# Two tiles of w2 on 32 partitions, in loads of six rows: a change to the last feed-forward of a two-layer decode kernel

## The chip, the cores and the metric

The kernel runs on one core of a Trainium2 chip. The metric is the device time of one execution in microseconds; lower is better. The core has TensorE (PE in the profile, its weight loads PEld), VectorE (DVE), ScalarE (ACT), GpSimd (POOL) and SyncE (SP), which issues nearly all DMAs here, and 16 DMA engines that move the data.

## The reference

Two layers of the same weights, each an attention block and a gated feed-forward, for 4 batch rows of one token (B=4, D=512, 32 query heads over 8 key heads, 4096 cached positions of 128 values, F=1792), all in float32:

```python
x = x + attention(layernorm(x), k_cache, v_cache, wq, wo)
x = x + (silu(h @ w1) * (h @ w3)) @ w2        # h = layernorm(x)
# ... and both lines once more, with the same caches and weights
```

Both layers read the whole k and v caches, 67 MB each. Together with the weights the core reads 298.33 MB from HBM and does little arithmetic on each byte.

## The kernel before

**The plan of loads.** All big operands go through one SBUF buffer, `arena` (218 units of 1 KB on each of 128 partitions). Lines 86 to 159 write out a list, `plan`, of every load of the run in the order in which SP is to issue them: source, size, and the pieces that the consumers will ask for. `cache()` cuts one head's k or v (64 units) into parts, `weights()` cuts a weight matrix. `pump()` (L164) walks the list: it asks `take()` (L56) for a free stretch of the arena, issues the DMA from SP (L183), and stops when nothing fits. `done()` (L196) frees a load's stretch when all of its pieces have been used, and pumps again. So the order of all big transfers is the order of the plan, and what holds a load back is free space in the arena.

**The units.** One unit is 256 floats, 1 KB per partition. An ordinary load lies on 128 partitions. A tile of w2 is 128 rows of h times 512 columns, two units, 256 KB; w2 has 14 of them (`WT`).

**The loads of the last layer.** After the last heads come w1 and w3 in two parts each (16 units, 16, 12, 12) and then w2. The first tile of w2 does not come on 128 partitions. It comes as `w2s`: 16 rows (`FEW`) of 16 KB each. Row r of it holds rows r, 16+r, 32+r and so on of the tile, side by side, so that the 256 KB lie on 16 partitions in 16 units of arena. Lines 150 to 153 cut them into four loads of four rows each (rows i, i+4, i+8, i+12), and lines 155 to 158 put one of them ahead of each of the four parts of w1 and w3. `pump()` takes 16 units for all of them at the first and has GpSimd clear them on all 128 partitions (L175); the loads themselves are issued at L177. The other 13 tiles follow as one list of parts of 8, 8, 4, 4 and 2 units (L159), that is 4, 4, 2, 2 and 1 tiles.

**The last feed-forward on TensorE.** `product()` makes w1 and w3 times x in two column parts (L530). After the first part of the gated h is there, L583 transposes it, and L586 cuts the 128 rows that belong to tile 0 into eight groups of `FEW` values on `FEW` partitions. `few(0, 4)` and `few(4, 8)` multiply these with the eight blocks of `w2s`, ahead of the last part of w3 and behind it; `columns()` (L555) writes four matmuls for each block or tile, one for each 128 output columns (L557). Then the loop at L615 takes tiles 1 to 13 as their loads land, with two idle matmuls (`busy`) after tiles 4 and 8. L670 copies the sum out of PSUM and L671 stores it.

**Where the first layer's FF uses w2.** Layer 0 loads all 14 tiles of w2 on 128 partitions in pairs and multiplies them in `down()` (L548).

**The k loads at the change of layers.** For the second head of layer 1 line 144 cuts k into loads of 8, 8, 8, 8, 16 and 16 units, for the third head into two of 32, and it leaves the later ones whole.

Of the kernel before, what the change touches and what calls it, by code (L numbers as in the profile page):

```python
# [13 lines left out]
B, D, HQ, HKV, SK, DH, F = 4, 512, 32, 8, 4096, 128, 1792  # L14
LAYERS = 2
REP = HQ // HKV
P = 128
# [6 lines left out]
FA = 2 * P  # L24
FB = FJ - FA
WT = 14
FEW = 16
EPS = 1e-5
SCALE = DH ** -0.5

KB = 256
# [7 lines left out]
def tile_decode_layers(ctx: ExitStack, tc: tile.TileContext, x, kt, v, wq, wo, w1, w3, w2, w2s, out):  # L39
# [46 lines left out]
    plan = []  # L86

    def load(src, per, keys, at=None):
        plan.append((src, per, keys, at))

    def cache(which, layer, g, parts, skip=0):
        src = (kt if which == "k" else v)[g]
        r = 8 * skip
        for n in parts:
            at = KEPT + r if (which, layer, g) in (("v", 0, TURN), ("k", 1, TURN - 2)) else None
            load(src[:, r * KB:(r + n) * KB], 8, [(which, layer, g, r // 8 + j) for j in range(n // 8)], at)
            r += n

    def weights(name, src, layer, parts, per, at=None, first=0):
        r = 0  # L100
        for n in parts:
            load(src[:, r * KB:(r + n) * KB], per, [(name, layer, first + r // per + j) for j in range(n // per)],
                 None if at is None else at + r)
            r += n

    order = [list(range(HKV)), list(reversed(range(HKV)))]
# [34 lines left out]
    ring["to"] = len(plan) - 1  # L141
    cache("k", 1, TURN, (8, 8, 16), SPLIT)
    for n in range(1, HKV):
        cache("k", 1, order[1][n], {1: (8, 8, 8, 8, 16, 16), 2: (32, 32)}.get(n, (64,)))
        if n > 1:
            cache("v", 1, order[1][n - 1], (32, 32) if n == HKV - 1 else (64,))
    cache("v", 1, 0, (32, 16, 16))


    side = iter([(w2s[i::4], slice(i, FEW, 4)) for i in range(4)])  # L150

    def aside():
        plan.append((*next(side), "few", None))

    for part, per, at in (("a", 4, 0), ("b", 3, 16)):
        for name, w in (("w1", w1), ("w3", w3)):
            aside()
            weights(name + part, w[:, at * KB:(at + 4 * per) * KB], 1, (4 * per,), per)
    weights("w2", w2[:, 2 * KB:], 1, (8, 8, 4, 4, 2), 2, None, 1)  # L159

    state = {"next": 0}
    where, left = {}, {}
# [29 lines left out]
    def loaded(*key):  # L192
        a, n, _ = where[key]
        return arena[:, a * KB:(a + n) * KB]

    def done(*key):  # L196
        i = where[key][2]
        k, a, n = left[i]
        left[i] = (k - 1, a, n)
        if k == 1:  # L200
            give(a, n)
            pump()
# [12 lines left out]
    few = const.tile([P, 4], F32, name="few")  # L215
# [37 lines left out]
    a = scaled  # L253
# [6 lines left out]
    hT = qT.rearrange("p h c -> p (h c)")[:, 0:(WT + 8) * B].rearrange("p (m b) -> p m b", b=B)  # L260
# [28 lines left out]
    def busy(n=1):  # L289

        while n > 0:
            w = min(n, 2)
            nc.tensor.matmul(m_ps[0:32, (4 - w) * P:], rows, ident.unsqueeze(1).broadcast_to([P, w, P]),  # L293
                             start=True, stop=True)
            n -= w
# [13 lines left out]
    def squares():  # L309
        sq = work.tile([P, KC, B], F32, name="sq", bufs=1)  # L310
        nc.vector.tensor_tensor(sq, xc, xc, op=ALU.mult)
        return sq

    def deviation(sq, m):
        var = small("var")
        nc.vector.scalar_tensor_tensor(sq, m, 1.0, pick, op0=ALU.mult, op1=ALU.mult, accum_out=var)
        nc.vector.tensor_scalar(var, var, EPS, None, op0=ALU.add)
        rstd = small("rstd")
        nc.gpsimd.tensor_tensor(rstd, var, half, op=ALU.pow)
        return rstd  # L320
# [164 lines left out]
    def pair(i, left, w, first, last):  # L485

        for n in range(2):
            for e in range(2):
                r = 32 * (2 * n + (e ^ (i % 2)))
                nc.tensor.matmul(x_ps[r:r + B, e * 256:e * 256 + 256], left(2 * i + n), w(n)[:, e * 256:e * 256 + 256],  # L490
                                 start=first, stop=last)
# [30 lines left out]
    def feed_forward(layer, mean):  # L522
        keep = layer < LAYERS - 1
        h = p[:, 0:FJ]

        def product(name, ps, lo, n, fill=(0, 0, 0, 0), ks=range(KC)):
            for k in ks:
                w = loaded(name, layer, k)
                for j in range(4):
                    nc.tensor.matmul(ps[32 * j:32 * j + 32, lo:lo + n], x32[:, k, :], w[:, j * n:(j + 1) * n],  # L530
                                     start=(k == 0), stop=(k == KC - 1))
                done(name, layer, k)
                busy(fill[k] if keep else 0)

        def gate(lo, n):
            a = h[:, lo:lo + n]
            nc.scalar.activation(a, s_ps[:, lo:lo + n], AF.Sigmoid, scale=rstd)
            nc.vector.scalar_tensor_tensor(a, s_ps[:, lo:lo + n], rstd, a, op0=ALU.mult, op1=ALU.mult)

        def join(lo, n):  # L540
            a = h[:, lo:lo + n]
            nc.vector.scalar_tensor_tensor(a, o_ps[:, lo:lo + n], rstd, a, op0=ALU.mult, op1=ALU.mult)

        def tiles(lo, n):
            slots = t_ps.rearrange("p i (j b) -> p (i j) b", j=4)
            nc.vector.tensor_copy(hT[:, lo:lo + n, :], slots[:, lo:lo + n, 0:B])

        def down(i):  # L548
            ws = [loaded("w2", layer, 2 * i + n) for n in range(2)]
            pair(i, lambda m: hT[:, m, :], lambda n: ws[n], i == 0, i == WT // 2 - 1)  # L550
            for n in range(2):
                done("w2", layer, 2 * i + n)
            busy((1, 2, 2, 2, 1, 2, 0)[i])

        def columns(rows, m, w, last=False):  # L555
            for k in range(KC):
                nc.tensor.matmul(x_ps[32 * k:32 * k + B, 0:P], hT[rows, m, :], w[rows, k * P:(k + 1) * P],  # L557
                                 start=False, stop=last)

        def few(lo, hi):  # L560
            for u in range(lo, hi):
                at = (where["few"] + 2 * u) * KB
                columns(slice(0, P), WT + u, arena[:, at:at + 2 * KB])

        sq = squares()
        product("w1a", s_ps, 0, FA, (0, 0, 2, 0))
        rstd = deviation(sq, total(flat(sq)))
        mean()
        if not keep:
            nc.vector.tensor_tensor(xt, xc, mu.unsqueeze(1).broadcast_to([P, KC, B]), op=ALU.add)  # L570
        product("w3a", o_ps, 0, FA, (2, 2, 2, 2))
        if not keep:
            for k in range(KC):
                nc.tensor.matmul(x_ps[32 * k:32 * k + B, 0:P], xt[:, k, :], ident, start=True, stop=False)
            busy(4)
        gate(0, FA)
        join(0, FA)
        product("w1b", s_ps, FA, FB, (1, 1, 1, 1))
        if keep:
            gate(FA, FB)  # L580
            nc.scalar.activation(spare, half, AF.Exp)
        for i in range(2):
            nc.tensor.transpose(t_ps[:, i, :], h[:, i * P:(i + 1) * P], ident)  # L583
        if not keep:
            for u in range(8):
                nc.tensor.matmul(t_ps[0:FEW, 2, B * u:B * u + B], h[0:32, FEW * u:FEW * u + FEW], ident[0:32, 0:B],  # L586
                                 start=True, stop=True)
            busy()
        tiles(0, 8)
        if not keep:  # L590
            nc.vector.tensor_copy(hT[0:FEW, WT:WT + 8, :], t_ps[0:FEW, 2, 0:8 * B].rearrange("p (u b) -> p u b", b=B))
            gate(FA, FB)
            few(0, 4)
        product("w3b", o_ps, FA, FB, (1, 2, 1, 1), range(0, 2))
        if keep:
            down(0)
        product("w3b", o_ps, FA, FB, (1, 2, 1, 1), range(2, KC))
        join(FA, FB)

        def tail_tiles():  # L600
            nc.tensor.transpose(t_ps[:, 2, :], h[:, FA:FA + P], ident)
            for u in (0, 64):
                nc.tensor.matmul(t_ps[u:u + 64, 3, 0:64], h[u:u + 64, FA + P:FJ], ident[u:u + 64, u:u + 64],
                                 start=True, stop=True)
            tiles(8, 6)

        if keep:
            for i in range(1, WT // 2):
                if i == 4:
                    tail_tiles()  # L610
                down(i)
            return
        few(4, 8)
        tail_tiles()
        for m in range(1, WT):  # L615
            columns(slice(0, P), m, loaded("w2", layer, m), m == WT - 1)
            done("w2", layer, m)
            if m in (4, 8):
                busy(2)
# [92 lines left out]
```

## Time and profile before

| | |
|---|---|
| median of 3 runs | 704.82 us (704.65 to 704.92) |
| profiled execution | 704.5 us, of which its span is 702.7 us |
| read from HBM | 298.33 MB, 425 GB/s over the span |
| PE busy, PEld, DVE, ACT, POOL | 402.9, 135.5, 85.2, 38.0, 7.0 us |

The span is the time from the first to the last instruction of the profiled execution. Busy times of engines overlap. Lines such as L557 are lines of the kernel before.

### The profile page before, as it was taken

The numbers are of one execution on the slowest core, as the hardware profiler recorded it, in microseconds if no ns is written. First come the engines' busy times: TensorE is split into PE (matmuls) and PEld (weight loads), VectorE is DVE, ScalarE is ACT, GpSimd is POOL, SyncE is SP. The second block draws the span as 40 slices with busy tenths as digits, with TensorE's granted clock in tenths as the row PEclk, the third lists the DMA queues.
The fourth block names the chain that finished last, engine by engine and source line by source line (L and its number), as shares of the span: only waits on it lengthen the run. The fifth ranks groups of instructions, "written<-read, shape, count | busy, mean of one in ns | idle before, by whom it ended". The sixth has DMA issues, their size and how long they took to land. (4 is left out here: it accounts for less than half of the span.)

```text
span 702.7 us, 7079 instructions
## 1 busy us (share of the span) xinstructions
PE 402.9 (57%) x3172; PEld 135.5 (19%) x3172; DVE 85.2 (12%) x291; ACT 38.0 (5%) x87; POOL 7.0 (1%) x12
## 2 busy tenths in 40 slices
PE   2555453555555454447888884365564545467677
PEld 1112011111111111112233321011120111122234
DVE  2001010101001010101111111020010101010111
ACT  0000000000000000102001000000000000000100
POOL 0000000000000000000000000000000000001000
PEclk9986787767778777779999997588787878788899
DMA  9999999999999999999999999999999999999997
GB/s 418 429 407 466 422 422 422 451 426 425 430 451 422 429 430 444 425 421 427 415 405 408 416 437 441 448 425 419 452 433 425 422 451 426 433 419 432 420 426 287
DMA packets 13174, 298.85 MB, mean 425 GB/s; under 512 B 1608, under 2 KB 1736, under 8 KB 6216
## 3 DMA queue, kind: packets, MB, share of 16 engines
q1 hardware_dynamic: 13008, 298.39, 99.2%
q8 instruction: 25, 0.41, 0.2%
q14 instruction: 6, 0.04, 0.0%
q10 hardware_dynamic: 135, 0.01, 0.0%
HBM read 298.33 MB, written 0.07 MB: 425 GB/s over the span
## 5 line engine op out<-in xcount | busy, mean ns | idle before, releaser
L462 PE MATMUL o_ps<-arena 128*32 128x512 f32 x1024 | 143.1, 706 | 149.6 <-DMA arena<-in_v 137.7
L415 PE MATMUL s_ps<-arena,qpad 128*32 128x512 f32 x1020 | 147.5, 732 | 92.0 <-DMA arena<-in_kt 92.0
L462 PEld LDWEIGHTS o_ps<-arena 128*32 128x32 f32 x1024 | 37.0, 127 | 253.3 <-issue 224.3
L415 PEld LDWEIGHTS s_ps<-arena,qpad 128*32 128x32 f32 x1020 | 39.3, 131 | 183.9 <-issue 176.4
L471 DVE SCALAR_TENSOR_TENSOR p<-o_ps,parts,p 128x512 f32<-128x512 f32 x16 | 12.0, 751 | 267.4 <-PE o_ps L462 267.4
L425 DVE TENSOR_REDUCE top<-s_ps 128x1 f32<-128x512 f32 x16 | 11.1, 691 | 196.6 <-PE s_ps L415 196.6
L469 ACT ACTIVATE p<-o_ps,parts 128x512 f32<-128x512 f32 x16 | 11.0, 687 | 188.5 <-PE o_ps L462 182.3
L293 PE MATMUL m_ps<-ident,rows 128*32 128x256 f32 (+1 forms) x84 | 20.9, 352 | 0.0
L353 PE MATMUL o_ps<-arena,xpad 128*32 128x512 f32 x112 | 15.5, 676 | 7.8 <-DMA arena<-in_wq 7.8
L448 PE MATMUL t_ps<-ident,p 128*128 128x128 f32 x64 | 10.9, 295 | 13.5 <-ACT p L442 13.5
L475 PE MATMUL t_ps<-ident,p 128*128 128x128 f32 x64 | 10.5, 287 | 13.9 <-DVE p L471 13.8
L435 ACT ACTIVATE f<-d 128x1 f32<-128x1 f32 x16 | 3.2, 203 | 251.0 <-DVE d L433 251.0
L497 PE MATMUL x_ps<-arena,qT 128*4 128x512 f32 x112 | 13.8, 592 | 5.1 <-DVE qT L483 3.6
L442 ACT ACTIVATE p<-s_ps,top 128x512 f32<-128x512 f32 x16 | 10.9, 684 | 75.9 <-PE t_ps L475 75.9
L449 DVE COPY arena<-t_ps 128x512 f32<-128x512 f32 x16 | 11.1, 691 | 9.3 <-PE t_ps L448 9.3
L475 PEld LDWEIGHTS t_ps<-ident,p 128*128 128x128 f32 x64 | 6.7, 140 | 28.0 <-DVE p L471 28.0
L448 PEld LDWEIGHTS t_ps<-ident,p 128*128 128x128 f32 x64 | 7.0, 145 | 22.2 <-ACT p L442 19.2
L293 PEld LDWEIGHTS m_ps<-ident,rows 128*32 128x32 f32 x84 | 9.0, 110 | 9.0 <-issue 3.5
L530 PE MATMUL s_ps<-arena,xpad 128*32 128x192 f32 (+1 forms) x128 | 7.9, 359 | 1.5 <-DMA arena<-in_w 1.5
L530 PE MATMUL o_ps<-arena,xpad 128*32 128x192 f32 (+1 forms) x128 | 8.1, 359 | 1.0 <-DMA arena<-in_w 0.9
L490 PE MATMUL x_ps<-arena,qT 128*4 128x256 f32 x88 | 6.6, 379 | 2.4 <-DMA arena<-in_w 1.7
L353 PEld LDWEIGHTS o_ps<-arena,xpad 128*32 128x32 f32 x112 | 3.5, 121 | 17.2 <-DMA arena<-in_wq 8.7
(108 smaller groups left out, 147.6 us busy)
## 6 DMA issues: line engine op xcount, KB each, us to landing
arena<-in_v SPq DMA_DIRECT2D x5, 4096.0 KB, 38.4
arena<-in_w SPq DMA_DIRECT2D x17, 512.0 KB, 9.3
arena<-in_kt SPq DMA_DIRECT2D x2, 4096.0 KB, 18.7
arena<-in_wq SPq DMA_DIRECT2D x1, 7168.0 KB
arena<-in_kt SPq DMA_DIRECT2D x6, 1024.0 KB, 11.2
arena<-in_kt SPq DMA_DIRECT2D x3, 2048.0 KB, 16.7
arena<-in_wo SPq DMA_DIRECT2D x1, 4096.0 KB, 24.0
arena<-in_v SPq DMA_DIRECT2D x2, 2048.0 KB, 36.9
```

The costliest lines, as they stand in the source:

```text
L293: nc.tensor.matmul(m_ps[0:32, (4 - w) * P:], rows, ident.unsqueeze(1).broadcast_to([P, w, P]), start=True, stop=True)
L353: nc.tensor.matmul(ps[32 * k:32 * k + 32, :], xpad[:, 32 * k + lo:32 * k + lo + 32], w[:, k, :], start=first, stop=last)
L415: nc.tensor.matmul(s_ps[32 * b:32 * b + 32, :], qpad[:, 32 * b + lo:32 * b + lo + 32], k[:, j, :], start=(blk == 0), stop=(blk == NB - 1))
L425: nc.vector.tensor_reduce(top[:, 0:1], s_ps, axis=AX.X, op=ALU.max, negate=True)
L448: nc.tensor.transpose(t_ps[:, i, :], p[:, i * P:(i + 1) * P], ident)
L449: nc.vector.tensor_copy(pT.rearrange("p i r -> p (i r)"), t_ps.rearrange("p i r -> p (i r)"))
L462: nc.tensor.matmul(o_ps[32 * b:32 * b + 32, :], pT[:, i, 32 * b:32 * b + 32], w[:, b, :], start=(i == 0), stop=(i == NI - 1))
L469: nc.scalar.activation(p, o_ps, AF.Copy, scale=st["parts"][:, 0:1])
L471: nc.vector.scalar_tensor_tensor(p, o_ps, st["parts"][:, 1:2], p, op0=ALU.mult, op1=ALU.add)
L475: nc.tensor.transpose(t_ps[:, j, :], p[:, j * P:(j + 1) * P], ident)
L497: nc.tensor.matmul(x_ps[r:r + B, :], left(2 * i + n), w(n), start=first, stop=False)
L530: nc.tensor.matmul(ps[32 * j:32 * j + 32, lo:lo + n], x32[:, k, :], w[:, j * n:(j + 1) * n], start=(k == 0), stop=(k == KC - 1))
```

## The change

Two tiles of w2 instead of one are laid as rows of 16 KB: the first 256 rows of h's first quarter, tiles 0 and 4, on 32 partitions (`FEW` = 32). Each of the eight blocks that `few()` multiplies now holds 32 rows. The 32 rows come in six loads, five of six consecutive rows and one of two: two loads ahead of the first part of w1 and two ahead of the first part of w3, one ahead of each second part. `TILE` keeps the list of w2's tiles in the order 0, 4, 1, 2, 3, 5, ...; the array in HBM is laid in that order, `down()` and the last loop look up h through it. The last loop runs over 12 tiles, loaded in parts of 8, 8, 6 and 2 units: 4, 4, 3 and 1 tiles. The third and fourth load of k for the second head of layer 1 become one of 16 units. The number of DMAs of the program is the same: two more for `w2s`, one less for w2, one less for k.

```diff
-FEW = 16
+FEW = 32
+TILE = (0, 4, 1, 2, 3, *range(5, WT))
...
-        cache("k", 1, order[1][n], {1: (8, 8, 8, 8, 16, 16), 2: (32, 32)}.get(n, (64,)))
+        cache("k", 1, order[1][n], {1: (8, 8, 16, 16, 16), 2: (32, 32)}.get(n, (64,)))
...
-    side = iter([(w2s[i::4], slice(i, FEW, 4)) for i in range(4)])
-
-    def aside():
-        plan.append((*next(side), "few", None))
+    side = [slice(6 * i, min(6 * i + 6, FEW)) for i in range(6)]
+
+    def aside(n):
+        for _ in range(n):
+            part = side.pop(0)
+            plan.append((w2s[part], part, "few", None))
...
-            aside()
+            aside(2 if part == "a" else 1)
             weights(name + part, w[:, at * KB:(at + 4 * per) * KB], 1, (4 * per,), per)
-    weights("w2", w2[:, 2 * KB:], 1, (8, 8, 4, 4, 2), 2, None, 1)
+    weights("w2", w2[:, 4 * KB:], 1, (8, 8, 6, 2), 2, None, 2)
...
-            pair(i, lambda m: hT[:, m, :], lambda n: ws[n], i == 0, i == WT // 2 - 1)
+            pair(i, lambda m: hT[:, TILE[m], :], lambda n: ws[n], i == 0, i == WT // 2 - 1)
...
-        for m in range(1, WT):
-            columns(slice(0, P), m, loaded("w2", layer, m), m == WT - 1)
+        for m in range(2, WT):
+            columns(slice(0, P), TILE[m], loaded("w2", layer, m), m == WT - 1)
...
-        "w2": lay(np.concatenate([full, rest], axis=1)).reshape(P, WT * D),
-        "w2s": lay(w2j[0, :P].reshape(8, FEW, D).transpose(1, 0, 2)).reshape(FEW, 8 * D),
+        "w2": lay(np.concatenate([full, rest], axis=1)[:, list(TILE)]).reshape(P, WT * D),
+        "w2s": lay(w2j[0, :FEW * 8].reshape(8, FEW, D).transpose(1, 0, 2)).reshape(FEW, 8 * D),
```

## The prediction

> **What bounds the kernel now.** I read the page first: busy shares, the forty slices, the DMA queues.
>
> ```profile
> span 702.7 us, 7079 instructions
> ...
> PE 402.9 (57%) x3172; PEld 135.5 (19%) x3172; DVE 85.2 (12%) x291; ACT 38.0 (5%) x87; POOL 7.0 (1%) x12
> ...
> DMA  9999999999999999999999999999999999999997
> ...
> q1 hardware_dynamic: 13008, 298.39, 99.2%
> ...
> q10 hardware_dynamic: 135, 0.01, 0.0%
> ```
>
> The sixteen DMA engines are full in 39 of 40 slices, and SP's queue q1 alone fills 99.2% of their time; TensorE is busy 57%. The kernel lasts as long as the transfers last, plus what follows the last byte. An edit counts only if it changes the bytes (this one doesn't), starves the engines, moves work between them at the end, or lengthens what comes behind the last landing. So I went to the end: the chain of waits in order of time, then the share of busy DMA engines in short windows.
>
> ```profile
> 683.82 15.04 DMA arena<-in_w
> 698.86 0.04 issue
> 698.90 0.62 PE x_ps L557 x16
> 699.52 0.02 issue
> 699.55 0.45 PE x_ps L557 x8
> 699.99 0.02 issue
> 700.02 0.29 DVE p L670
> ```
>
> ```profile
> 660.00:680.00 20.00, 14.43 (x117) 5.51 (x117) 3.70 (x11) 3.24 (x7) 0.00 (x0) 1.00 0.99 420
> ...
> 694.00:695.00 1.00, 1.00 (x37) 0.96 (x34) 0.18 (x1) 0.00 (x0) 0.00 (x0) 1.00 0.98 373
> 695.00:696.00 1.00, 0.49 (x6) 0.01 (x1) 0.00 (x0) 0.00 (x0) 0.00 (x0) 1.00 0.75 299
> 696.00:697.00 1.00, 0.62 (x24) 0.61 (x28) 0.00 (x0) 0.00 (x0) 0.00 (x0) 1.00 0.75 293
> 697.00:698.00 1.00, 1.00 (x34) 0.71 (x26) 0.00 (x0) 0.00 (x0) 0.00 (x0) 1.00 0.57 229
> 698.00:699.00 1.00, 0.38 (x16) 0.10 (x8) 0.00 (x0) 0.00 (x0) 0.00 (x0) 1.00 0.42 145
> 699.00:700.00 1.00, 0.93 (x24) 0.34 (x19) 0.00 (x0) 0.00 (x0) 0.00 (x0) 1.00 0.00 0
> ```
>
> In a window row the last columns are granted clock, DMA share and GB/s. The chain says that the load ahead of the last one ends the last long wait: it lands at 698.86, sixteen matmul records (two tiles) take 0.62, the last tile 0.45 from 699.55, then copy and store. The windows show how the engines run out: 0.75 of 16 is 12 still busy from 695 to 697, 0.57 is nine until 698, and by 699 nothing moves. So four engines finish about 695, three more about 697, nine between 698.3 and 699.
>
> This gives a first bound. The idle shares from 694 to 699 add up to 0.02 + 0.25 + 0.25 + 0.43 + 0.58 = 1.53 us. Were all sixteen to finish together, the last byte would land 1.53 us earlier: 0.22% of 704.8. No rebalancing of the end can give more. About 0.2%, 1.4 us, is also what a measurement of this kernel can tell from no change.
>
> **Which engines carry the 16 KB rows.** A load of 120 rows (x, line 210, the only load of queue q10) left 135 packets: 120 rows and 15 closing ones, so it ran on 15 engines, one closing packet for each. With the same count q1's 13,008 are 90 transfers of 128 rows (128 + 16 each), x's first 8 rows (8 + 8), and 32 for the four w2s loads, which is four times 4 + 4. So a load of four rows ran on four engines, one row each; six rows should run on six engines and two on two, since a number of rows that is no power of two (120) was split by its largest divisor. [...]
>
> The trace also holds each packet's start and length. Chained end to start, an estimate of mine beside the windows, they give sixteen ends: four chains hold all sixteen 16 KB rows, so it was the same four engines each time, and they end near 696.9, 696.9, 697.1 and 699.05. Of the twelve others four end at 694.5 to 696.0, and eight at 698.3 to 698.8. That fits the windows.
>
> **The parts, priced.** A 16 KB row: 420 GB/s at a share of 0.99 is 26.5 GB/s for an engine, so 0.62 us. A w2 tile on 128 partitions is 8 rows of 2 KB, 16 KB, on every engine: from 695 to 696, 299 GB/s on 12 engines is 24.9 each, 0.66 us.
>
> *All sixteen engines* lose one tile: -0.66. *The four engines with rows now* carry 4 rows, 2.48 us. After it the first two of the six carry 5 + 1 rows and the next two 5: +1.24 - 0.66 = +0.58 for two and +0.62 - 0.66 = -0.04 for two. *Two engines more* take 5 rows: +3.10 - 0.66 = +2.44. If these two are among the early four, they end at 696.9 to 698.4; if among the late eight, at 701.2. *The ten others* gain 0.66; the late eight end at 697.6 to 698.2.
>
> So all hangs on two identities. That the two newcomers are early I take as likely: the early eight are the four row carriers (without rows they would end near 694.4 to 696.6) and four others, and engines side by side in the order of use are likelier to share the cause than to be split by it. Which of the carriers ends at 699.05 decides the last byte: third or fourth in the order 699.0, first or second 699.6. By count that is even. I take 699.0, because one of the four early chains without rows is late in its group too (696.0, the others 694.5 to 695.0): if lateness touches neighbours, the pair is the fourth carrier and the first newcomer.
>
> *Behind the last byte.* The last two loads are now three tiles and one, where they were two and one. A tile costs 0.31:
>
> ```profile
> 697.65 0.64 PE L557 MATMUL x_ps<-arena,qT 128*4 128x128 f32 x16
> 698.90 1.04 PE L557 MATMUL x_ps<-arena,qT 128*4 128x128 f32 x24 [0.62 <-DMA arena<-in_w]
> ```
>
> Two tiles in 0.64. The last tile still lands about 0.65 behind the load before it; two tiles just filled that gap (698.90 to 699.52), three need 0.94. So the last tile starts 0.3 later: +0.3. Twelve tiles instead of thirteen spare TensorE 0.31, but ahead of a wait, so nothing.
>
> *SP's queue.* The issues of the last loads:
>
> ```profile
> 644.01 0.70 SPq L177 DMA_DIRECT2D arena<-in_w2s  x1
> 644.76 0.43 SPq L183 DMA_DIRECT2D arena<-in_w  x1
> 645.24 0.61 SPq L177 DMA_DIRECT2D arena<-in_w2s  x1
> 645.96 0.38 SPq L183 DMA_DIRECT2D arena<-in_w  x1
> 654.47 0.60 SPq L177 DMA_DIRECT2D arena<-in_w2s  x1
> 664.20 0.33 SPq L183 DMA_DIRECT2D arena<-in_w  x1
> 669.09 0.60 SPq L177 DMA_DIRECT2D arena<-in_w2s  x1
> 674.03 10.60 SPq L183 DMA_DIRECT2D arena<-in_w  x6
> ```
>
> The steps 9.73, 4.89 and 4.94 are the times of a load of 4 MB and two of 2 MB: v's last three parts, which land one after the other. Counted along the plan, each issue waits until the load eight places ahead has landed. With two more w2s loads in front, w3's first part moves from 645.96 to 664.2 and w1's second part from 664.20 to 674.03, w3's to about 675. Behind them only SP's later issues are queued. The cover: the DMA engines must still have work then. The first parts of w1 and w3, 2 MB each, wait in the ring from about 645 and 664; they are 9.8 us of transfer by the steps above. The late engines reach them at 674, the early ones some 4 us before, at 670, so these run dry only at 679.8; w1's second part is there 5 us earlier. Price nothing; if that cover were gone, each microsecond of delay would cost the early engines alone, which end 2 to 4 us ahead. The issue itself, 0.6 each, lies beside transfers.
>
> *The k loads.* One load of 16 units waits for space that two of 8 got one k block apart:
>
> ```profile
> 391.82 1.04 PE L415 MATMUL s_ps<-arena,qpad 128*32 128x512 f32 x8
> ...
> 393.54 1.04 PE L415 MATMUL s_ps<-arena,qpad 128*32 128x512 f32 x8
> ```
>
> ```profile
> arena<-in_kt SPq DMA_DIRECT2D x6, 1024.0 KB, 11.2
> ```
>
> A block takes 1.72, so the issue slips by at most about that. In the list of DMA issues a load of 1 MB lands 11.2 after its issue, though it takes 2.5 by itself: some 8.7 us of backlog cover it. Price nothing, 1.7 without cover.
>
> *The rest* goes together: eight transposing matmuls write 32 rows instead of 16, one DVE copy has 32 rows, GpSimd clears the same stretch; `few()` waits for six loads, the last of them ahead of w3's second part, which is needed 1 us later. All of it lies ahead of the wait for w2.
>
> **Sum.** Last byte 699.05 to 699.0, last tile +0.3: +0.25. Against the profiled execution (704.5; span 702.7, 1.8 around it) that is 704.75; the median lies 0.3 above the profiled run, so 705.0.
>
> **Rivals.** *The last carrier is one of the first two*: last byte +0.58, tail +0.3: 705.7. For it only the even count. Chance 0.2.
>
> *The late carrier isn't late in the new order.* It ends 2 us behind its three fellows, and no view shows why; whatever holds it up may fall elsewhere. Then the newcomer at 698.4 is last: -0.65, tail +0.3, so 704.8 - 0.35, about 704.5. Chance 0.2.
>
> *Slower: the newcomers are late engines.* They end at 701.2 instead of 698.8, 2.2 behind today's last byte; with the tail 704.8 + 2.2 + 0.3 = 707.3. It decides from an engine that ends after 696.6 today. Against it that four of the twelve engines without rows are early. [...] Chance 0.12.
>
> *Not what it says: six rows on two engines* (a power of two). Sixteen rows each are 9.9 against 2.5 now, and a tile less: +6.8 on carriers that end near 697 to 699, so 703.7 to 705.8 and a time of about 710. The 15 engines of q10 speak against it. Chance 0.03.
>
> **How the numbers follow.** The forecast, 705.0, has 0.42, the two small rivals 0.2 each, the slower one 0.12, the split 0.03; 0.03 is left for a starved queue. The first three span 704.5 to 705.7; with 0.3 of scatter, 704.2 to 706.0 hold some 0.8. Faster by over 0.2% would need 703.4, nearly the whole 1.53 us: 0.04. Slower by over 0.2%, above 706.2: 0.14. Same: 0.82.
>
> **What would show it.** Right: in the windows, a share from 695 to 697 above 0.75, since the newcomers fill the early end, and a last nonzero window within 0.7 us of 699; in the chain, a last-but-one wait that ends near 698.8, then 24 records of L557 in about 0.94 and the last tile behind them without a wait; q1 with 88 x 144 + 16 + 64 = 12,752 packets (32 rows and 6 x 5 + 2 closing ones). Wrong: transfers past 700 on two engines (a share near 0.13), which would be late newcomers; a share under 0.95 anywhere between 380 and 690, which would be starvation; a w1 or w3 wait of TensorE over 1 us.

## The result, and the profile after

The changed kernel takes 712.67 us (median of 4 runs, 712.53 to 714.0) against 704.75 us (4 runs, 704.65 to 704.92). The ratio is 1.0116, 95% interval 1.0103 to 1.0128: slower by 7.9 us. The forecast was 705.0, with 706.0 as its upper end, and no rival stood at this value.

The profiled execution took 712.53 us. From its page (line numbers after the change are three higher than before in the lines shown here):

```profile
span 710.8 us, 7061 instructions
...
DMA  9999999999999999999999999999999999999995
GB/s 414 428 421 446 414 450 425 428 447 424 429 443 421 435 440 420 440 420 424 411 405 406 426 436 462 424 413 462 418 417 462 417 425 457 414 419 438 395 339 203
...
q1 hardware_dynamic: 12752, 298.39, 98.6%
```

q1 has the 12,752 packets that were worked out, so the loads did run on six and on two engines, and the bytes are the same. The engines are as busy as before, but in slices 38 and 39 they move 395 and 339 GB/s. A busy share alone hides this: the packets take longer. Short windows (span, then busy times of PE, PEld, DVE, ACT and POOL, then granted clock, DMA share and GB/s) show where it begins:

```profile
668.00:670.00 2.00, 0.95 (x12) 0.43 (x16) 0.00 (x0) 0.69 (x1) 0.00 (x0) 1.00 1.08 410
670.00:672.00 2.00, 2.00 (x18) 0.72 (x10) 0.00 (x0) 0.00 (x0) 0.00 (x0) 1.00 0.98 377
672.00:674.00 2.00, 0.22 (x2) 0.00 (x0) 0.00 (x0) 0.00 (x0) 0.00 (x0) 1.00 0.98 336
...
678.00:680.00 2.00, 1.50 (x12) 0.66 (x14) 1.06 (x3) 0.00 (x0) 0.00 (x0) 0.97 1.01 229
680.00:682.00 2.00, 2.00 (x22) 0.94 (x15) 0.44 (x3) 0.48 (x2) 0.00 (x0) 1.00 0.83 309
...
684.00:686.00 2.00, 2.00 (x34) 1.23 (x32) 0.00 (x0) 0.00 (x0) 0.00 (x0) 1.00 1.02 324
686.00:688.00 2.00, 0.53 (x4) 0.34 (x3) 0.87 (x6) 0.47 (x1) 0.55 (x1) 1.00 0.96 319
```

The rate falls from about 670, the time at which the prediction has the early engines reach the loads behind the first 16 KB rows, and it dips again several times up to 692. At 678 to 680 all sixteen engines are busy at 229 GB/s, 14 each instead of 26.5. If only the six that carry rows had stood still, the ten others would have moved 265. The trace's own packets say the same: the 44 packets of 16 KB that were under way in these two microseconds took 0.96 to 1.53 us each, where the median in the kernel before (660 to 680) is 0.61. So every engine was slowed.

On TensorE the waits for w1 and w3 show the same. From the timeline of PE, first the product with the first part of w3 in the kernel before, then the changed kernel:

```profile
684.19 1.93 PE L530 MATMUL o_ps<-arena,xpad 128*32 128x256 f32 x32
```

```profile
683.89 1.93 PE L533 MATMUL s_ps<-arena,xpad 128*32 128x256 f32 x32 [0.70 <-DMA arena<-in_w]
...
691.19 3.64 PE L533 MATMUL o_ps<-arena,xpad 128*32 128x256 f32 x32 [4.38 <-DMA arena<-in_w]
...
696.51 1.51 PE L533 MATMUL s_ps<-arena,xpad 128*32 128x192 f32 x32 [0.37 <-DMA arena<-in_w]
```

TensorE waits 4.38 us for the first part of w3, and the product starts 7 us later than before. It takes 3.64 us instead of 1.93, at a granted clock of 0.50. TensorE doesn't set the end, though: the chain of waits, in order of time, still ends on a load of w2.

```profile
685.37 21.52 DMA arena<-in_w
706.89 0.04 issue
706.93 1.10 PE x_ps L560 x32
708.03 0.02 issue
708.06 0.29 DVE p L673
```

The load of three tiles lands at 706.89; the load before the last landed at 698.86 before. That is 8.03 us, nearly all of the 8.1 by which the span grew. In the windows the engines run out one after the other, and from 705 to 707 hardly more than one of the sixteen (a share of 0.06) is still at work:

```profile
701.00:702.00 1.00, 1.00 (x36) 0.86 (x32) 0.18 (x1) 0.00 (x0) 0.00 (x0) 1.00 0.53 205
...
703.00:704.00 1.00, 1.00 (x36) 0.81 (x35) 0.18 (x1) 0.00 (x0) 0.00 (x0) 1.00 0.22 76
...
706.00:707.00 1.00, 0.60 (x13) 0.18 (x10) 0.00 (x0) 0.00 (x0) 0.00 (x0) 1.00 0.06 23
```

### The profile page after: what moved, and what is told of

The parts are those of the page before. It is cut to its first block, busy times and chain, and to the rows that moved or that the text cites. A ratio compares the mean times of both kernels' runs of the same rounds, so it can differ in the third digit from the quotient of the medians.

```text
span 710.8 us, 7061 instructions
## 1 busy us (share of the span) xinstructions
PE 409.8 (58%) x3164; PEld 137.6 (19%) x3164; DVE 85.2 (12%) x291; ACT 38.0 (5%) x87; POOL 7.0 (1%) x12
## 3 DMA queue, kind: packets, MB, share of 16 engines
q1 hardware_dynamic: 12752, 298.39, 98.6%
## 5 line engine op out<-in xcount | busy, mean ns | idle before, releaser
L465 PE MATMUL o_ps<-arena 128*32 128x512 f32 x1024 | 146.4, 720 | 150.0 <-DMA arena<-in_v 138.3
L533 PE MATMUL o_ps<-arena,xpad 128*32 128x192 f32 (+1 forms) x128 | 9.8, 422 | 5.3 <-DMA arena<-in_w 5.2
```

The costliest lines, as they stand in the source:

```text
L465: nc.tensor.matmul(o_ps[32 * b:32 * b + 32, :], pT[:, i, 32 * b:32 * b + 32], w[:, b, :], start=(i == 0), stop=(i == NI - 1))
```

## The experiments

Three theories stood first. A: neighbouring partitions written at once slow the transfers. B: neighbouring rows of 16 KB read at once from HBM do. C: neither; the split by six or the engines new to these rows are the cost.

| run | median us | ratio to before, 95% interval |
|---|---|---|
| every fifth row, both sides | 711.78 | 1.0101 (1.0086 to 1.0116) |
| every fifth partition only | 712.42 | 1.0108 (1.0093 to 1.0123) |
| every fifth HBM row only | 712.76 | 1.0110 (1.0093 to 1.0126) |
| before, four neighbours | 710.39 | 1.0079 (1.0064 to 1.0094) |
| before, on partitions 64 to 79 | 708.76 | 1.0057 (1.0039 to 1.0075) |
| before, on partitions 32 to 47 | 704.86 | 1.0000 (0.9991 to 1.0010) |
| 32 rows, four loads of eight | 706.04 | 1.0017 (1.0007 to 1.0026) |
| 32 rows, six-row loads, every fourth partition | 706.62 | 1.0029 (1.0017 to 1.0041) |
| before, fifth row empty | 704.75 | 0.9999 (0.9990 to 1.0008) |
| before, fifth and sixth row empty | 706.45 | 1.0025 (1.0016 to 1.0034) |
| before, last loads three tiles and one | 704.74 | 1.0001 (0.9992 to 1.0010) |
| before, HBM neighbours, same partitions | 704.74 | 1.0000 (0.9991 to 1.0009) |

The kernel before measured 704.68 to 704.84 beside them.

**Every fifth row, on both sides.**

```diff
-    side = [slice(6 * i, min(6 * i + 6, FEW)) for i in range(6)]
+    side = [slice(i, 30, 5) for i in range(5)] + [slice(30, FEW)]
```

> The changed kernel, but each load of six takes every fifth row (i, i+5, ... i+25; then rows 30 and 31) instead of six neighbours, in HBM and on the partitions alike, as the loads of four in the kernel before took every fourth. Same loads, sizes, engines and order. Theory A (neighbouring partitions written at once slow the transfers) and theory B (neighbouring 16 KB rows read at once from HBM slow them) both expect about 705, within 704.2 to 706.0 as forecast, and a DMA rate of 420 GB/s from 660 to 680 us instead of 375. Theory C (the split by six, or the engines that are new to these rows, are the cost) expects 712 to 713 as the change has.

It took 711.78: only 0.9 less than the change. Theories A and B fall in the form stated.

**Every fifth partition only, and every fifth HBM row only.** The slices above on one side, the old ones on the other; the host orders the array's rows to match.

> The changed kernel with only the partitions spread: each load still reads six neighbouring rows of HBM, but writes them to every fifth partition (the host lays the array's rows so that the right ones come). Theory A expects about 705, as when both sides are spread; theory B expects 712 to 713, no gain; theory C 712 to 713.

> The changed kernel with only the rows in HBM spread: each load reads every fifth row and writes six neighbouring partitions. Theory A expects 712 to 713, no gain; theory B expects about 705; theory C 712 to 713.

712.42 and 712.76. By themselves the three runs would leave theory C.

**The kernel before with four neighbours.**

```diff
-    side = iter([(w2s[i::4], slice(i, FEW, 4)) for i in range(4)])
+    side = iter([(w2s[4 * i:4 * i + 4], slice(4 * i, 4 * i + 4)) for i in range(4)])
```

> The kernel before with its four loads of four rows taken as neighbours (0 to 3, 4 to 7, ...) instead of every fourth row, in HBM and on the partitions. Theories A and B expect it slower, by about half of the change's 7.9 us since half as many rows are read or written side by side: 707 to 709. Theory C expects 704.8, since neither the split nor the engines differ.

710.39: 5.7 us from the choice of rows alone, with the old split, the old engines and one tile. So C falls as well, as the whole cause. Something about rows i, i+4, i+8, i+12 is cheap that six neighbours, four neighbours and every fifth row all lack.

That led to theory D: what counts is on which partitions a load's rows land, not which rows of HBM they are. The author expected 707 to 711 for the kernel before on partitions 64 to 79 and 704.7 on 32 to 47; both rested on an assumption about which engine writes which partitions, and no view shows that. The two runs that follow measure the places themselves, and the rival for the first, that only rows of one load that lie close to each other clash, expected 704.7. Every fifth row speaks against that rival already: the six rows of a load lie five apart, on partitions 0 to 31, and the run took 711.78 all the same.

**Partitions 64 to 79, and 32 to 47.** The kernel before, its 16 rows moved as a block; the small transposing matmuls and their copy write there too.

```diff
-    side = iter([(w2s[i::4], slice(i, FEW, 4)) for i in range(4)])
+    side = iter([(w2s[i::4], slice(LOW + i, LOW + FEW, 4)) for i in range(4)])
...
```

> After the first four runs theories A and B fall as stated: spreading by five rows helps neither on the partitions, nor in HBM, nor on both, yet the kernel before becomes slow with four neighbours. [...] This run is the kernel before with its 16 rows on partitions 64 to 79 instead of 0 to 15, the same loads of every fourth row on the same engines. [...]

> The kernel before with its 16 rows on partitions 32 to 47. [...] A theory that any partitions but the first 16 are dear expects what the run on 64 to 79 shows.

708.76 and 704.86. The two differ in nothing but the partitions (`LOW` is 64 or 32), and rows four apart are no protection. Sixteen rows cost 3.9 us on 64 to 79 and 5.7 as four neighbours on 0 to 15; why these two prices differ, no run shows. The slow one's windows show the low rates, at a full share:

```profile
670.00:672.00 2.00, 2.00 (x19) 0.70 (x12) 0.00 (x0) 0.00 (x0) 0.00 (x0) 1.00 0.98 328
...
676.00:678.00 2.00, 1.47 (x12) 0.67 (x7) 0.88 (x2) 0.00 (x0) 0.00 (x0) 1.00 0.96 311
...
682.00:684.00 2.00, 1.90 (x34) 0.96 (x25) 0.06 (x1) 0.00 (x0) 0.00 (x0) 1.00 0.97 295
```

**32 rows in loads of eight, every fourth row.**

```diff
-    side = [slice(6 * i, min(6 * i + 6, FEW)) for i in range(6)]
+    side = [slice(i, FEW, 4) for i in range(4)]
...
-            aside(2 if part == "a" else 1)
+            aside(1)
```

> The changed kernel with its 32 rows in four loads of eight, every fourth row (0, 4, ... 28; then 1, 5, ...), one ahead of each part of w1 and w3; two loads fewer than the change has. [...] Theory D expects no slow stretch (420 GB/s from 660 to 690 us) and 705 to 707: the two engines that are new and end late gain 2.48 - 1.3 = 1.2 us. Theory C (two tiles on 32 rows are dear whatever the rows) expects 711 to 713.

706.04: two tiles on 32 rows are not dear in themselves. The rate is 422 GB/s from 660 to 680 and 419 from 680 to 690, where the change has 375 and 356.

**Six-row loads on every fourth partition.** The change with four loads of six rows on partitions i, i+4, ... i+20 and one of eight on 32, 36, ... 60; the eight small transposing matmuls become sixteen, and the rows of h and of w2s are permuted to match:

```diff
-    side = [slice(6 * i, min(6 * i + 6, FEW)) for i in range(6)]
+    side = [(slice(i, 24, 4), slice(i, 24, 4)) for i in range(4)]
+    side += [(slice(24, 32), slice(32, 61, 4))]
...
-            aside(2 if part == "a" else 1)
+            aside(2 if (part, name) == ("a", "w1") else 1)
...
-                nc.tensor.matmul(t_ps[0:FEW, 2, B * u:B * u + B], h[0:32, FEW * u:FEW * u + FEW], ident[0:32, 0:B],
+                nc.tensor.matmul(t_ps[0:24, 2, B * u:B * u + B], h[0:32, 64 + 24 * u:88 + 24 * u], ident[0:32, 0:B],
+                                 start=True, stop=True)
+                lo = 32 * (u // 4) + u % 4
+                nc.tensor.matmul(t_ps[32:61, 2, B * u:B * u + B], h[0:32, lo:lo + 29], ident[0:32, 0:B],
...
```

> [...] Theory D expects 704.2 to 706.0, the forecast that stood on an undisturbed DMA rate; theory C expects 711 to 713.

706.62 (six executions, 706.26 to 708.00): 6.05 us less than the change, and the slow stretch is gone, as its windows show:

```profile
670.00:672.00 2.00, 1.82 (x17) 0.60 (x18) 0.00 (x0) 0.13 (x1) 0.00 (x0) 1.00 1.00 426
672.00:674.00 2.00, 1.38 (x10) 0.48 (x5) 0.00 (x0) 0.00 (x0) 0.00 (x0) 1.00 1.00 418
...
678.00:680.00 2.00, 1.74 (x20) 0.54 (x18) 0.79 (x4) 0.00 (x0) 0.00 (x0) 1.00 1.04 440
```

But theory D's expectation of 704.2 to 706.0 was missed by 0.6. At a full rate w1's second part was still late (lines of this kernel are four higher than before):

```profile
690.21 2.33 PE L534 MATMUL s_ps<-arena,xpad 128*32 128x192 f32 x32 [2.68 <-DMA arena<-in_w]
```

In the kernel before the same product began at 687.57:

```profile
687.57 1.51 PE L530 MATMUL s_ps<-arena,xpad 128*32 128x192 f32 x32 [0.39 <-DMA arena<-in_w]
```

The 2.6 us between them are about four rows of 16 KB. That asked for theory L: one of the two new engines is one of the late ones.

The same profile, of the slowest of the six executions (708.00), has a second cause in it. Behind that wait TensorE's granted clock is 0.50 from 694 to 697, a group of 32 records takes 1.89 us where the same group took 1.06 in the kernel before, and from 690.21 to the end the chain of waits holds no load any more:

```profile
694.00:695.00 1.00, 1.00 (x16) 0.59 (x18) 0.61 (x3) 0.00 (x0) 0.00 (x0) 0.50 0.89 369
```

```profile
694.47 1.89 PE L561 MATMUL x_ps<-arena,qT 128*4 128x128 f32 x32
```

```profile
690.08 0.14 issue
690.21 2.33 PE s_ps L534 x32
...
702.20 1.16 PE x_ps L561 x32
703.35 0.02 issue
703.38 0.29 DVE p L677
```

So in this execution TensorE set the end, about two microseconds after the last packet of w2 (701.21). How much of the median of 706.62 is the clock and how much the late engine, this run alone does not say.

**A fifth row, a fifth and a sixth row, empty.** The kernel before with rows of zeros added (partitions 16 to 19, or 16 to 23, so that each load stays on every fourth partition), to load an engine without changing anything else; the zeros add nothing to the sum. The edit for both rows, where the run with the fifth alone has 20 in place of 24 and the host adds the rows of zeros:

```diff
-    side = iter([(w2s[i::4], slice(i, FEW, 4)) for i in range(4)])
+    side = iter([(w2s[i::4], slice(i, 24, 4)) for i in range(4)])
...
```

> The run with aligned six-row loads (706.6) is still 1.8 above the kernel before, and its load of w1's second part landed 2.5 us later (690.1 against 687.5) at a full DMA rate, which is four 16 KB rows. Theory L: one of the two engines that are new to these rows is one of those that end late anyway. Rival T: the engines are early, and the rest of the change (the last loads of three tiles and one, the merged k load) costs the 1.8. This run is the kernel before with a fifth row in each of the four loads, on partitions 16 to 19, filled with zeros: the fifth engine gets 4 rows, 2.48 us, and nothing else changes. If the fifth engine is an early one: 704.8. If it is a late one (ends at 698.8 before): 701.3 for the last byte, about 707. Rival T expects 704.8.

> The same with a fifth and a sixth row of zeros (partitions 16 to 23), so that the fifth and the sixth engine get 4 rows each. Theory L expects about 707 here, since one of the two is late, and the run with five rows tells which. Rival T expects 704.8.

704.75 and 706.45. The fifth engine takes four rows for nothing; the sixth costs 1.7 us. The windows of the run with both have about one engine at work (a share of 0.06 to 0.10) for more than a microsecond behind all others, and the last long wait in its chain ends at 701.20, 2.34 us later than in the kernel before (698.86):

```profile
699.00:700.00 1.00, 1.00 (x33) 0.72 (x29) 0.00 (x0) 0.00 (x0) 0.00 (x0) 1.00 0.14 55
700.00:701.00 1.00, 0.61 (x17) 0.32 (x16) 0.00 (x0) 0.00 (x0) 0.00 (x0) 1.00 0.06 25
701.00:702.00 1.00, 0.73 (x21) 0.43 (x24) 0.00 (x0) 0.00 (x0) 0.00 (x0) 1.00 0.10 25
```

```profile
684.27 16.93 DMA arena<-in_w
701.20 0.04 issue
701.24 0.62 PE x_ps L557 x16
```

**The change's other edits to the loads alone**, on the kernel before:

```diff
-    weights("w2", w2[:, 2 * KB:], 1, (8, 8, 4, 4, 2), 2, None, 1)
+    weights("w2", w2[:, 2 * KB:], 1, (8, 8, 2, 6, 2), 2, None, 1)
...
-        cache("k", 1, order[1][n], {1: (8, 8, 8, 8, 16, 16), 2: (32, 32)}.get(n, (64,)))
+        cache("k", 1, order[1][n], {1: (8, 8, 16, 16, 16), 2: (32, 32)}.get(n, (64,)))
```

> The kernel before with the change's other edits alone: the last two loads of w2 hold three tiles and one (parts 8, 8, 2, 6, 2), and the third and fourth k load of the second head are one. The prediction's step says +0.3 for the tail and nothing for the k load: 705.1. Rival T expects 706.6. Theory L alone expects 704.8 to 705.1.

704.74: nothing. The chain of this run:

```profile
698.98 0.04 issue
699.03 1.10 PE x_ps L557 x32
700.13 0.02 issue
```

Four tiles behind the wait take 1.10 us in one piece. Before, two tiles, a wait and one tile took 1.09, from 698.90 to 699.99.

**Neighbouring rows of HBM, the old partitions.**

```diff
-    side = iter([(w2s[i::4], slice(i, FEW, 4)) for i in range(4)])
+    side = iter([(w2s[4 * i:4 * i + 4], slice(i, FEW, 4)) for i in range(4)])
```

> The kernel before with each load reading four neighbouring rows of HBM, and writing them to the same partitions as before (i, i+4, i+8, i+12; the host lays the array's rows to match). Theory D, that only the partition counts, expects 704.8. The rival, that neighbouring rows in HBM are a part of the 5.7 us that four neighbours on both sides cost, expects 706 to 708.

704.74. Reading neighbours from HBM costs nothing; of the 5.7 us of the four neighbours nothing is left for the source.

## Why the prediction was wrong

**The step that failed** is the price of a 16 KB row: 0.62 us, taken from a stretch in which the rows of each load lay on every fourth partition from 0 to 15. The prediction counted rows per engine and never asked which partitions they land on, although the diff changes just that (`w2s[i::4]` to `6 * i` and on). In the slow stretch, from 678 to 680, a packet of 16 KB took 0.96 us and more, on all engines. The runs put 6.05 of the 7.9 us on it: the change against the same kernel with its rows moved to every fourth partition (712.67 against 706.62; that run has one load fewer and eight more small matmuls, and its executions spread over 1.7 us, so the figure is good to about 1 us).

The end of the transfers says it without TensorE: the last packet of w2 ends at 699.04 before, at 707.04 after the change, at 701.21 with the six-row loads on every fourth partition. The shares of the windows from 694 on, added up, give an estimate of where the engines end on average: 697.5, 701.7 and 697.5. So some 4.2 of the 8.0 us are the slow stretch, which all engines lose, and 2.2 are the late newcomer. The other 1.6 are an end more uneven still than in that run, and no run takes them apart further.

Shown is that the partition decides (708.76 on 64 to 79 against 704.86 on 32 to 47) and the HBM side doesn't (704.74). What makes one partition dearer than another the runs do not show, nor why the engines without rows slow down too, as the 229 GB/s say.

**The newcomers** were the step that the prediction called uncertain, and the slower rival was half right: the fifth engine is an early one (704.75 with a fifth row), the sixth a late one (706.45 with a sixth). Its price was near: that rival had the last byte at 701.2, and with the six-row loads on every fourth partition it comes at 701.21. The run with a sixth row has its last long wait end 2.34 us later; in the median that is 1.7 us.

**Behind the last byte** the +0.3 was mis-sized; it is nothing measurable. A tile was priced at half of 0.64 us, but that row holds two tiles and something that comes once per group. 32 records take 1.06 and 24 take 0.84 in the timelines of PE of the change:

```profile
705.06 0.84 PE L560 MATMUL x_ps<-arena,qT 128*4 128x128 f32 x24 [0.52 <-DMA arena<-in_w]
...
706.93 1.06 PE L560 MATMUL x_ps<-arena,qT 128*4 128x128 f32 x32 [0.40 <-DMA arena<-in_w]
```

So a tile (8 records) costs 0.22, and 0.18 comes once per group. Three tiles then take 0.66 before the next can follow, and the gap is 0.65.

**What held.** The split by six and two (12,752 packets). The bound by transfers and the reading of the end. The k load at no cost. SP's queue: w1's second part was to be issued at 674.03 and w3's at about 675, and the trace has 674.35 and 676.25:

```profile
674.35 0.35 SPq L186 DMA_DIRECT2D arena<-in_w  x1
675.18 0.23 SPq L180 DMA_DIRECT2D arena<-in_w2s  x1
676.25 15.28 SPq L186 DMA_DIRECT2D arena<-in_w  x5
```

The sign that was named for starvation, a share under 0.95 before 690, shows in one of the short windows from 668 to 690 (0.83 from 680 to 682), behind the slowest stretch. It is worth 0.34 us at most. Two other signs of being wrong came true: a wait for w3 of 4.38 us, and transfers long past 700, at the last on one engine.

**The bound.** That no rebalancing could bring more than 1.53 us agrees with every run, since none was measurably faster than the kernel before, but no run tests it. By its estimates a better version would be hard to measure: the fifth engine has room, but the late ones, which set the end, gain only a tile's 0.66 us for every tile that moves away from them.

## What to carry to other kernels

A load on few partitions is priced by where its rows land, not only by its bytes and its number of engines. Here loads of up to eight rows on every fourth partition, from one of 0 to 3 on or from one of 32 to 35 on, ran at 420 to 426 GB/s from 660 to 680, where the change has 375; neighbours on 0 to 15 cost 5.7 us, and every fourth partition from one of 64 to 67 on cost 3.9. Where such a load is slow, the same load on other partitions is the run to make. When a DMA share near 1 goes with a lower GB/s (here 1.01 with 229), look at the partitions of the rows before looking for starvation. Before work is shifted to idle engines, load one of them with rows that nobody needs and see whether the end moves.

## What the runs showed of the hardware

- Sixteen rows of 16 KB, 0.09% of the bytes, cost 3.9 us more on partitions 64 to 79 (708.76) than on 0 to 15 (704.84), and nothing more on 32 to 47 (704.86).
- Rows next to each other in a load differ in price: a fifth row in each of the four loads is free (704.75 against 704.78), and a sixth one costs 1.7 us (706.45). What makes some engines end some 4 us behind others in the kernel before is not settled here.
- A DMA share of 1.01 went with 229 GB/s (the change, 678 to 680), where 1.00 went with 423 in the kernel before (670 to 680): a busy share near 1 does not show that the engines move data at their full rate.
- TensorE's granted clock was 0.50 when it went on after its wait of 4.38 us in the slow kernel (690 to 695), where it was 1.00 in the kernel before, and again behind the wait of 2.68 us in the run with the six-row loads on every fourth partition (694 to 697):

```profile
690.00:694.00 4.00, 2.81 (x28) 1.38 (x32) 0.00 (x0) 0.00 (x0) 0.00 (x0) 0.50 0.99 350
694.00:695.00 1.00, 1.00 (x16) 0.48 (x9) 0.10 (x1) 0.00 (x0) 0.00 (x0) 0.50 1.06 444
```
